# VectorE's tile loop in a group normalisation: from one tile per trip with addresses in registers to six slots per trip with fixed addresses

One core of one Trainium2 chip runs the kernel. The metric is the device time of one execution in microseconds (us). The kernel is hand-scheduled: each engine has its own program, and semaphores tie them together.

## The reference

Group normalisation of 128 samples, 1024 channels in 32 groups, 32 x 16 pixels, in bf16:

```python
xr = x.reshape(B, G, C // G, H, W)                       # 128, 32, 32, 32, 16
mu = xr.mean(axis=(2, 3, 4), keepdims=True)
var = ((xr - mu) ** 2).mean(axis=(2, 3, 4), keepdims=True)
xn = (xr - mu) / jnp.sqrt(var + 1e-5)
return xn.reshape(B, C, H, W) * g[None, :, None, None] + b[None, :, None, None]
```

## The kernel before

A tile is four samples: 128 partitions (sample and group) x 16384 elements, 4.19 MB. There are 32 tiles and a ring of six slots in SBUF. A tile is loaded into its slot, reduced, normalised in place and stored. SyncE issues every load and store into one queue, in batches (RUNS): some stores, then as many loads into the slots that they free. TensorE adds up the first half of a tile in PSUM; VectorE adds up the second half in one instruction (the *pair sum*); ScalarE turns both into the mean, squares the tile and makes the standard deviation; VectorE inverts it, makes scale and bias for 32 channels and runs 32 multiplies over the tile.

VectorE's program, the part that is changed, is a loop with one tile per trip. The slot depends on the trip, so the addresses are computed into registers:

```python
def part(i, lo, n):
    at = (i % SLOTS) * (F * ITEM) + lo * ITEM
    return bytes_of_ring[:, bass.ds(at, n * ITEM)].bitcast(BF16)

def pair(i):
    e.wait_ge(first_in, i + 1)                # TensorE's first matmul of tile i
    e.scalar_tensor_tensor(out=jp[:], in0=part(i, lo, n), scalar=1.0, in1=part(i, lo + n, n),
        ..., accum_out=ps[:, bass.ds((i % PS_BUFS) * (2 * MM_FREE) + MM_FREE, 1)]).then_inc(paired, 1)
...
pair(0)
with nc.Fori(0, NT, 1, engines=[e.engine]) as i:
    with e.If(i < NT - 1):
        e.drain()
        pair(i + 1)                           # one tile ahead
    parts = [part(i, k * HW, HW) for k in range(KC)]
    e.wait_ge(stded, i + 1)                   # ScalarE
    e.reciprocal(out=rstd[:], in_=std[:, bass.ds(i % SLOTS, 1)]).then_inc(inverted, 1)
    ...                                       # scale, bias
    for k, a in enumerate(parts):             # 32 multiplies
        ts = e.tensor_scalar(out=a, in0=a, ...)
        if (k + 1) % KQ == 0:
            ts.then_inc(done, 1)              # four times a tile; SyncE's stores wait for it
```

SyncE's stores and loads, unchanged:

```python
def load(j):
    if j >= SLOTS:
        e.wait_ge(st[j % SLOTS], ...)         # the store that frees the slot has landed
    e.dma_start(out=slot(j), in_=x_v[j]).then_inc(ld[j % SLOTS], 16)
def store(i):
    w = F // store_parts(i)                   # one part; two for tile 2, four for the last
    for p in range(store_parts(i)):
        e.wait_ge(done, NQ * i + NQ // store_parts(i) * (p + 1))
        e.dma_start(out=o_v[i][:, p * w : (p + 1) * w], in_=slot(i)[:, p * w : (p + 1) * w]).then_inc(...)
```

Of the kernel before, what the change touches and what calls it, by code (L numbers as in the profile page):

```python
# [8 lines left out]
ALU = mybir.AluOpType  # L9
F32 = mybir.dt.float32  # L10
BF16 = mybir.dt.bfloat16
# [5 lines left out]
SLOTS = 6  # L17
RUNS = (3, 4, 4, 4, 4, 4, 3, 6)
NQ = 4
PS_BUFS = 3  # L20
PE_CHUNKS = 16
MM_FREE = 512
# [35 lines left out]
def kernel(  # L58
# [13 lines left out]
    nc = tc.nc  # L72
# [3 lines left out]
    HW = H * W  # L76
# [3 lines left out]
    NT = B0 // NS  # L80
    KC = C // G
    F = KC * HW
    inv_n = 1.0 / float(F)
    NMM = F // MM_FREE
    ROUNDS = -(-NT // SLOTS)
    REST = NT - (ROUNDS - 1) * SLOTS
    KQ = KC // NQ
    PAIRED = F - PE_CHUNKS * MM_FREE
    ITEM = 2
# [8 lines left out]
    def sbuf(name, shape, dtype):  # L98
        return nc.alloc_sbuf_tensor(name, shape, dtype)


    ring = sbuf("ring", [P, SLOTS * F], BF16)
    ja = sbuf("ja", [P, F // 2], FP8)
    jm = sbuf("jm", [P, MM_FREE + 1], FP8)
    jp = sbuf("jp", [P, PAIRED // 2], FP8)
# [4 lines left out]
    gb = sbuf("gb", [P, 2 * KC], F32)  # L110
    eps_t = sbuf("eps_t", [P, 1], F32)
    warm = sbuf("warm", [P, 1], F32)
    nm = sbuf("nm", [P, SLOTS], F32)
    sq = sbuf("sq", [P, 2], F32)
    var = sbuf("var", [P, 1], F32)
    std = sbuf("std", [P, SLOTS], F32)
    rstd = sbuf("rstd", [P, 1], F32)
    scl = sbuf("scl", [P, KC], F32)
    bia = sbuf("bia", [P, KC], F32)

    ps = nc.alloc_psum_tensor("ps", [P, PS_BUFS * 2 * MM_FREE], F32)
    gb_p = nc.alloc_psum_tensor("gb_p", [P, 2 * KC], F32)

    def sem(name):
        return nc.alloc_semaphore(name)

    def sems(name):
        return [sem(f"{name}{c}") for c in range(SLOTS)]

    ld, st, summed, meaned = (sems(n) for n in ("ld", "st", "sum", "mean"))  # L130

    half, both, varred = (sems(n) for n in ("half", "both", "var"))
    inverted, scaled, shifted = (sem(n) for n in ("inv", "scl", "bia"))
    first_in, paired, stded, done = (sem(n) for n in ("first", "pair", "std", "done"))
    s_gb, s_ones, s_eye, s_gbp, s_fin = (sem(n) for n in ("gbl", "ones", "eye", "gbp", "fin"))

    def store_parts(i):
# [2 lines left out]
    def slot(i):  # L140
        return ring[:, (i % SLOTS) * F : (i % SLOTS + 1) * F]

    def sums(c):
        return ps[:, c % PS_BUFS * 2 * MM_FREE : c % PS_BUFS * 2 * MM_FREE + MM_FREE]

    def sums_and_pairs(c):
        return ps[:, c % PS_BUFS * 2 * MM_FREE : c % PS_BUFS * 2 * MM_FREE + MM_FREE + 1]
# [49 lines left out]
    def in_rounds(e, one):  # L197
        with nc.Fori(0, ROUNDS, 1, engines=[e.engine]) as t:
            for c in range(REST):
                one(c, t)  # L200
            with e.If(t < ROUNDS - 1):
                for c in range(REST, SLOTS):
                    one(c, t)

    def on_tensor(e):
        e.wait_ge(s_eye, 2)
        e.wait_ge(s_gb, 32)
        e.matmul(out=gb_p[:], lhsT=rep[:], rhs=gb_b[:], start=True, stop=True).then_inc(s_gbp, 1)  # L208

        e.ldweights(eye[:])  # L210

        def add_up(to, chunk, k):
            return e.add_instruction(  # L213
                mybir.InstMatmult(
                    name=nc.get_next_instruction_name(),
                    engine=e.engine,
                    start_tensor_calc=(k == 0),
                    stop_tensor_calc=(k == PE_CHUNKS - 1),
                    ins=[e.lower_ap(chunk), e.lower_ap(eye[:])],
                    outs=[e.lower_ap(to)],  # L220
                    tile_size=(P, P),
                    tile_position=(0, 0),
                    ldweights=False,
                )
            )

        def one(c, t):
            for k in range(PE_CHUNKS):
                if k == 0:
                    e.wait_ge(ld[c], (t + 1) * 16)  # L230
                elif k == PE_CHUNKS - 2:

                    e.wait_ge(meaned[(c - 2) % SLOTS], t + 1)
                elif k == PE_CHUNKS - 1:
                    e.wait_ge(paired, t * SLOTS + (c + 1))
                mm = add_up(sums(c), slot(c)[:, k * MM_FREE : (k + 1) * MM_FREE], k)
                if k == 0:
                    mm.then_inc(first_in, 1)
            mm.then_inc(summed[c], 1)

        in_rounds(e, one)

    def on_scalar(e):
        e.dma_start(out=gb_b[:, 0:KC], in_=g_v).then_inc(s_gb, 16)
        e.dma_start(out=gb_b[:, KC : 2 * KC], in_=b_v).then_inc(s_gb, 16)
        e.wait_ge(s_ones, 1)
        e.activation(out=warm[:], in_=eps_t[:], func=ACT.Sqrt)  # L247

        def one(c, t):
            e.wait_ge(summed[c], t + 1)  # L250
            e.activation(  # L251
                out=jm[:], in_=sums_and_pairs(c), func=ACT.Identity, scale=-inv_n,
                accum_out=nm[:, c : c + 1], saturate=False,
            ).then_inc(meaned[c], 1)
            for h, (ready, at) in enumerate(
                ((meaned[c], t + (2 if c >= SLOTS - 2 else 1)), (half[c], t + 1))
            ):
                e.wait_ge(ready, at)
                e.activation(  # L259
                    out=ja[:],  # L260
                    in_=slot(c)[:, h * (F // 2) : (h + 1) * (F // 2)],
                    func=ACT.Square,
                    bias=nm[:, c : c + 1],
                    scale=1.0,
                    accum_out=sq[:, h : h + 1],
                    saturate=False,
                ).then_inc((half, both)[h][c], 1)
            e.wait_ge(both[c], t + 1)
            e.activation(  # L269
                out=var[:], in_=sq[:, 0:1], func=ACT.Identity, bias=eps_t[:], scale=inv_n  # L270
            ).then_inc(varred[c], 1)
            e.wait_ge(varred[c], t + 1)
            e.activation(  # L273
                out=std[:, c : c + 1], in_=sq[:, 1:2], func=ACT.Sqrt, bias=var[:], scale=inv_n
            ).then_inc(stded, 1)

        in_rounds(e, one)

    def on_vector(e):
        bytes_of_ring = ring[:].bitcast(mybir.dt.uint8)  # L280

        def part(i, lo, n):
            at = (i % SLOTS) * (F * ITEM) + lo * ITEM
            return bytes_of_ring[:, bass.ds(at, n * ITEM)].bitcast(BF16)

        def pair(i):
            lo, n = PE_CHUNKS * MM_FREE, PAIRED // 2
            e.wait_ge(first_in, i + 1)
            e.scalar_tensor_tensor(  # L289
                out=jp[:],  # L290
                in0=part(i, lo, n),
                scalar=1.0,
                in1=part(i, lo + n, n),
                op0=ALU.mult,
                op1=ALU.add,
                accum_out=ps[:, bass.ds((i % PS_BUFS) * (2 * MM_FREE) + MM_FREE, 1)],
                saturate=False,
            ).then_inc(paired, 1)

        e.wait_ge(s_gbp, 1)  # L300
        e.tensor_copy(out=gb[:], in_=gb_p[:])  # L301
        pair(0)
        with nc.Fori(0, NT, 1, engines=[e.engine]) as i:
            with e.If(i < NT - 1):
                e.drain()  # L305
                pair(i + 1)
            parts = [part(i, k * HW, HW) for k in range(KC)]
            e.keepalive_nop([e.lower_ap(a) for a in parts])  # L308
            e.wait_ge(stded, i + 1)
            e.reciprocal(out=rstd[:], in_=std[:, bass.ds(i % SLOTS, 1)]).then_inc(inverted, 1)  # L310
            e.wait_ge(inverted, i + 1)
            e.tensor_scalar(  # L312
                out=scl[:], in0=gb[:, 0:KC], scalar1=rstd[:], scalar2=None, op0=ALU.mult
            ).then_inc(scaled, 1)
            e.wait_ge(scaled, i + 1)
            e.scalar_tensor_tensor(  # L316
                out=bia[:], in0=scl[:], scalar=nm[:, bass.ds(i % SLOTS, 1)],
                in1=gb[:, KC : 2 * KC], op0=ALU.mult, op1=ALU.add,
            ).then_inc(shifted, 1)
            e.wait_ge(shifted, i + 1)  # L320
            for k, a in enumerate(parts):
                ts = e.tensor_scalar(  # L322
                    out=a, in0=a, scalar1=scl[:, k : k + 1], scalar2=bia[:, k : k + 1],
                    op0=ALU.mult, op1=ALU.add,
                )
                if (k + 1) % KQ == 0:
                    ts.then_inc(done, 1)

    with entry_block(tc) as entry:
        first_load(nc.sync)  # L330
# [3 lines left out]
        at = next(k for k, i in enumerate(rest) if is_drain(i) and i.engine == load_0.engine)  # L334
# [36 lines left out]
```

## Time and profile before

| | before |
|---|---|
| time, median of the first three runs | 630.68 us (630.53 to 631.03) |
| span in the profile | 629.1 us |
| DMA queue that carries the data | 268.44 MB, 99.3% of the engines' time |
| VectorE, ScalarE, TensorE busy | 497.2, 504.0, 187.5 us |

The profile's lines are shown in the prediction. In a line of groups or of the timeline, "busy" counts the engine alone; registers, branches, drains and waits of its sequencer are not in it. A row with a "q" behind the engine (DVEq, SPq) is such sequencer work. "A <- B" in a view of waits says what ended A's wait.

### The profile page before, as it was taken

Reading aid. Unit: us, or ns where it says so; the run is one execution under the profiler, and the core shown is the slowest. Engines: PE = TensorE matmul, PEld = TensorE weight load, DVE = VectorE, ACT = ScalarE, POOL = GpSimd, SP = SyncE. Lnnn points to the kernel's source line nnn. Section 1 sums busy time; section 2 is a strip of 40 time slices with the busy share of each in tenths; the row PEclk is TensorE's granted clock in tenths of the full one; section 3 lists DMA queues with packets and bytes.
Section 4 is the critical chain, followed back from the end, with each engine's and each line's share of the span. In section 5 each row is a group of like instructions: output and inputs, shape, how many; then the busy total and the mean of one; then the engine's idle time right before and its main releaser. Section 6 shows DMA issues by size and latency. Waiting matters only on the chain.

```text
span 629.1 us, 2702 instructions
## 1 busy us (share of the span) xinstructions
PE 187.5 (30%) x508; PEld 0.2 (0%) x2; DVE 497.2 (79%) x1185; ACT 504.0 (80%) x258; POOL 1.0 (0%) x8
## 2 busy tenths in 40 slices
PE   2533333430243303433024330343303333063000
PEld 0000000000000000000000000000000000000000
DVE  1479999999499982999829998299983999899962
ACT  0899999999589992999929999299991999979940
POOL 0000000000000000000000000000000000000000
PEclk9867766665577755777557775577755866577555
DMA  9999999999999999999999999999999999999996
GB/s 400 433 433 400 433 433 433 433 433 433 431 433 433 433 433 433 433 425 433 433 433 433 433 431 433 433 433 433 433 433 433 433 431 431 433 427 433 433 419 270
DMA packets 9888, 268.44 MB, mean 427 GB/s; under 512 B 1184, under 2 KB 1184, under 8 KB 1184
## 3 DMA queue, kind: packets, MB, share of 16 engines
q1 hardware_dynamic: 9792, 268.44, 99.3%
q10 hardware_dynamic: 96, 0.00, 0.0%
HBM read 134.22 MB, written 134.22 MB: 427 GB/s over the span
## 4 chain that ended last, share of the span: by engine, by line
ACT 32%; DVE 25%; DMA 24%; issue 9%; PE 4%; DVEq 3%; SPq 0%; ACTq 0%
ACT ja L259 30%; DVE ring L322 23%; DMA ring<-in_x_dram 22%; PE ps L213 4%; DMA gb_b<-in_b_dram 2%; ACT jm L251 1%; DVEq L305 1%; DVEq L308 1%; DVE jp L289 1%; ACT var L269 1%; ACT std L273 1%; DVE bia L316 1%; DVE scl L312 1%; DVEq L289 0%; DVE rstd L310 0%
## 5 line engine op out<-in xcount | busy, mean ns | idle before, releaser
L259 ACT ACTIVATE ja<-ring,nm 128x8192 fp8e5<-128x8192 bf16 x64 | 455.8, 7122 | 2.1
L322 DVE TENSOR_SCALAR ring<-ring,scl,bia x1024 | 333.7, 409 | 1.2
L213 PE MATMUL ps<-ring,eye 128*128 128x512 bf16 x507 | 187.3, 543 | 389.3 <-DVE jp L289 235.1
L289 DVE SCALAR_TENSOR_TENSOR jp<-ring 128x4096 fp8e5 (+1 forms) x32 | 141.6, 4425 | 80.9 <-PE ps L213 68.9
L251 ACT ACTIVATE jm<-ps 128x513 fp8e5<-128x513 f32 x32 | 19.2, 601 | 95.3 <-PE ps L213 95.3
L310 DVE RECIPROCAL rstd<-std 128x1 f32 x32 | 5.7, 177 | 19.3 <-ACT std L273 19.2
L259 ACT ACTIVATION_READ_ACCUMULATOR ja<-ring,nm 128x1 f32 x64 | 11.9, 186 | 0.0
L316 DVE SCALAR_TENSOR_TENSOR bia<-scl,nm,gb 128x32 f32<-128x32 f32 x32 | 8.0, 251 | 4.2
L301 DVE COPY gb<-gb_p 128x64 f32<-128x64 f32 x1 | 0.2, 225 | 12.8 <-PE gb_p L208 12.8
L273 ACT ACTIVATE std<-sq,var 128x1 f32<-128x1 f32 x32 | 9.4, 294 | 1.0
L269 ACT ACTIVATE var<-sq,eps_t 128x1 f32<-128x1 f32 x32 | 9.4, 295 | 1.0
L312 DVE TENSOR_SCALAR scl<-gb,rstd 128x32 f32<-128x32 f32 x32 | 7.7, 242 | 1.1
L251 ACT ACTIVATION_READ_ACCUMULATOR jm<-ps 128x1 f32 x32 | 6.2, 194 | 0.0
L289 DVE DVE_READ_ACCUMULATOR jp<-ring (+1 forms) x32 | 4.5, 142 | 0.0
L208 PE MATMUL gb_p<-gb_b,rep 32*128 32x64 bf16 x1 | 0.2, 208 | 12.5 <-DMA gb_b<-in_b_dram 12.5
L247 ACT ACT_TABLE_LOAD x1 | 1.3, 1283 | 1.8 <-PEq L355 1.8
L190 POOL TENSOR_SCALAR_AFFINE_SELECT rep<-ones_b 32x128 bf16<-32x128 bf16 x1 | 0.3, 303 | 0.0
L186 POOL TENSOR_SCALAR_AFFINE_SELECT eye<-ones_b 128x128 bf16<-128x128 bf16 x1 | 0.3, 293 | 0.4 <-issue 0.4
L247 ACT ACTIVATE warm<-eps_t 128x1 f32<-128x1 f32 x1 | 0.2, 203 | 0.0
L180 POOL MEMSET ones_b<- 128x128 bf16 x1 | 0.2, 204 | 0.3 <-POOLq L355 0.3
L210 PEld LDWEIGHTS <-eye 128*128 128x128 bf16 x1 | 0.1, 105 | 0.1
L208 PEld LDWEIGHTS gb_p<-gb_b,rep 32*128 32x128 bf16 x1 | 0.1, 100 | 12.5 <-issue 12.5
(5 smaller groups left out, 0.5 us busy)
## 6 DMA issues: line engine op xcount, KB each, us to landing
ring<-in_x_dram SPq DMA_DIRECT2D x32, 4096.0 KB, 36.8
out_dram<-ring SPq DMA_DIRECT2D x30, 4096.0 KB, 26.9
out_dram<-ring SPq DMA_DIRECT2D x2, 2048.0 KB, 12.5
out_dram<-ring SPq DMA_DIRECT2D x4, 1024.0 KB, 9.2
gb_b<-in_g_dram ACTq DMA_DIRECT2D x1, 2.0 KB, 7.8
gb_b<-in_b_dram ACTq DMA_DIRECT2D x1, 2.0 KB, 11.1
```

Source lines behind the costliest of these rows:

```text
L213: return e.add_instruction(mybir.InstMatmult(name=nc.get_next_instruction_name(), engine=e.engine, start_tensor_calc=(k == 0), stop_tensor ...
L251: e.activation(out=jm[:], in_=sums_and_pairs(c), func=ACT.Identity, scale=-inv_n, accum_out=nm[:, c : c + 1], saturate=False,).then_inc(me ...
L259: e.activation(out=ja[:], in_=slot(c)[:, h * (F // 2) : (h + 1) * (F // 2)], func=ACT.Square, bias=nm[:, c : c + 1], scale=1.0, accum_out= ...
L269: e.activation(out=var[:], in_=sq[:, 0:1], func=ACT.Identity, bias=eps_t[:], scale=inv_n).then_inc(varred[c], 1)
L273: e.activation(out=std[:, c : c + 1], in_=sq[:, 1:2], func=ACT.Sqrt, bias=var[:], scale=inv_n).then_inc(stded, 1)
L289: e.scalar_tensor_tensor(out=jp[:], in0=part(i, lo, n), scalar=1.0, in1=part(i, lo + n, n), op0=ALU.mult, op1=ALU.add, accum_out=ps[:, bas ...
L305: e.drain()
L308: e.keepalive_nop([e.lower_ap(a) for a in parts])
L310: e.reciprocal(out=rstd[:], in_=std[:, bass.ds(i % SLOTS, 1)]).then_inc(inverted, 1)
L312: e.tensor_scalar(out=scl[:], in0=gb[:, 0:KC], scalar1=rstd[:], scalar2=None, op0=ALU.mult).then_inc(scaled, 1)
L316: e.scalar_tensor_tensor(out=bia[:], in0=scl[:], scalar=nm[:, bass.ds(i % SLOTS, 1)], in1=gb[:, KC : 2 * KC], op0=ALU.mult, op1=ALU.add,). ...
L322: ts = e.tensor_scalar(out=a, in0=a, scalar1=scl[:, k : k + 1], scalar2=bia[:, k : k + 1], op0=ALU.mult, op1=ALU.add,)
```

## The change

The intent is to take loop overhead off VectorE: with one trip per *round* of six slots every address is a constant, so that the drain and the register arithmetic ahead of each tile can go. Each slot then has semaphores of its own, counted once per round. The pair sum also waits for the load itself instead of for TensorE's first matmul. Cut to its core:

```diff
-        def pair(i):
-            lo, n = PE_CHUNKS * MM_FREE, PAIRED // 2
-            e.wait_ge(first_in, i + 1)
+        def pair(c, turn):
+            first, w = PE_CHUNKS * MM_FREE, PAIRED // 2
+            e.wait_ge(ld[c], turn * 16)
             e.scalar_tensor_tensor(
                 out=jp[:],
-                in0=part(i, lo, n),
+                in0=slot(c)[:, first : first + w],
 ... (in1 and accum_out alike)
-            ).then_inc(paired, 1)
-        with nc.Fori(0, NT, 1, engines=[e.engine]) as i:
-            with e.If(i < NT - 1):
-                e.drain()
-                pair(i + 1)
-            parts = [part(i, k * HW, HW) for k in range(KC)]
-            e.keepalive_nop([e.lower_ap(a) for a in parts])
-            e.wait_ge(stded, i + 1)
-            e.reciprocal(out=rstd[:], in_=std[:, bass.ds(i % SLOTS, 1)]).then_inc(inverted, 1)
+            ).then_inc(paired[c], 1)
+        def one(c, t):
+            then = (c + 1) % SLOTS, t + (1 + (c + 1) // SLOTS)
+            if c == REST - 1:
+                with e.If(t < ROUNDS - 1):
+                    pair(*then)
+            else:
+                pair(*then)
+            e.wait_ge(stded[c], t + 1)
+            e.reciprocal(out=rstd[:], in_=std[:, c : c + 1]).then_inc(inverted[c], 1)
 ... (scale, bias and the 32 multiplies alike, with slot(c) for the register address)
+        in_rounds(e, one)      # a loop over six rounds, six slots in each
 ... (TensorE: the wait for `paired` per slot, `first_in` is gone; ScalarE: semaphores per slot)
```

More of the change, by code (lines that the diff above doesn't have):

```diff
@@ L128, in sems @@
         return [sem(f"{name}{c}") for c in range(SLOTS)]
-    ld, st, summed, meaned = (sems(n) for n in ("ld", "st", "sum", "mean"))
-    half, both, varred = (sems(n) for n in ("half", "both", "var"))
-    inverted, scaled, shifted = (sem(n) for n in ("inv", "scl", "bia"))
-    first_in, paired, stded, done = (sem(n) for n in ("first", "pair", "std", "done"))
+    ld, st, summed, paired, meaned, stded = (
+        sems(n) for n in ("ld", "st", "sum", "pair", "mean", "std")
+    )
+    half, both, varred, inverted, scaled, shifted = (
+        sems(n) for n in ("half", "both", "var", "inv", "scl", "bia")
+    )
+    done = sem("done")
     s_gb, s_ones, s_eye, s_gbp, s_fin = (sem(n) for n in ("gbl", "ones", "eye", "gbp", "fin"))
@@ L234, in one @@
                 elif k == PE_CHUNKS - 1:
-                    e.wait_ge(paired, t * SLOTS + (c + 1))
+                    e.wait_ge(paired[c], t + 1)
                 mm = add_up(sums(c), slot(c)[:, k * MM_FREE : (k + 1) * MM_FREE], k)
-                if k == 0:
-                    mm.then_inc(first_in, 1)
             mm.then_inc(summed[c], 1)
@@ L254, in one @@
             ).then_inc(meaned[c], 1)
-            for h, (ready, at) in enumerate(
-                ((meaned[c], t + (2 if c >= SLOTS - 2 else 1)), (half[c], t + 1))
-            ):
-                e.wait_ge(ready, at)
+            e.wait_ge(meaned[c], t + (2 if c >= SLOTS - 2 else 1))
+            for h in range(2):
+                if h == 1:
+                    e.wait_ge(half[c], t + 1)
                 e.activation(
@@ L266, in one @@
                     saturate=False,
-                ).then_inc((half, both)[h][c], 1)
+                ).then_inc(both[c] if h == 1 else half[c], 1)
             e.wait_ge(both[c], t + 1)
@@ L274, in one @@
                 out=std[:, c : c + 1], in_=sq[:, 1:2], func=ACT.Sqrt, bias=var[:], scale=inv_n
-            ).then_inc(stded, 1)
+            ).then_inc(stded[c], 1)
         in_rounds(e, one)
     def on_vector(e):
-        bytes_of_ring = ring[:].bitcast(mybir.dt.uint8)
-        def part(i, lo, n):
-            at = (i % SLOTS) * (F * ITEM) + lo * ITEM
-            return bytes_of_ring[:, bass.ds(at, n * ITEM)].bitcast(BF16)
-        def pair(i):
-            lo, n = PE_CHUNKS * MM_FREE, PAIRED // 2
-            e.wait_ge(first_in, i + 1)
+        e.wait_ge(s_gbp, 1)
@@ L289, in pair @@
+        e.tensor_copy(out=gb[:], in_=gb_p[:])
+        def pair(c, turn):
+            first, w = PE_CHUNKS * MM_FREE, PAIRED // 2
+            e.wait_ge(ld[c], turn * 16)
             e.scalar_tensor_tensor(
                 out=jp[:],
-                in0=part(i, lo, n),
+                in0=slot(c)[:, first : first + w],
                 scalar=1.0,
-                in1=part(i, lo + n, n),
+                in1=slot(c)[:, first + w : first + 2 * w],
                 op0=ALU.mult,
                 op1=ALU.add,
-                accum_out=ps[:, bass.ds((i % PS_BUFS) * (2 * MM_FREE) + MM_FREE, 1)],
+                accum_out=ps[:, c % PS_BUFS * 2 * MM_FREE + MM_FREE :][:, 0:1],
@@ L297, in pair @@
                 saturate=False,
-            ).then_inc(paired, 1)
-        e.wait_ge(s_gbp, 1)
-        e.tensor_copy(out=gb[:], in_=gb_p[:])
-        pair(0)
-        with nc.Fori(0, NT, 1, engines=[e.engine]) as i:
-            with e.If(i < NT - 1):
-                e.drain()
-                pair(i + 1)
-            parts = [part(i, k * HW, HW) for k in range(KC)]
-            e.keepalive_nop([e.lower_ap(a) for a in parts])
-            e.wait_ge(stded, i + 1)
-            e.reciprocal(out=rstd[:], in_=std[:, bass.ds(i % SLOTS, 1)]).then_inc(inverted, 1)
-            e.wait_ge(inverted, i + 1)
+            ).then_inc(paired[c], 1)
@@ L312, in on_vector @@
+        def one(c, t):
[7 more added lines that the diff above has]
+            e.reciprocal(out=rstd[:], in_=std[:, c : c + 1]).then_inc(inverted[c], 1)
+            e.wait_ge(inverted[c], t + 1)
             e.tensor_scalar(
                 out=scl[:], in0=gb[:, 0:KC], scalar1=rstd[:], scalar2=None, op0=ALU.mult
-            ).then_inc(scaled, 1)
@@ L315, in on_vector @@
-            e.wait_ge(scaled, i + 1)
+            ).then_inc(scaled[c], 1)
+            e.wait_ge(scaled[c], t + 1)
             e.scalar_tensor_tensor(
-                out=bia[:], in0=scl[:], scalar=nm[:, bass.ds(i % SLOTS, 1)],
-                in1=gb[:, KC : 2 * KC], op0=ALU.mult, op1=ALU.add,
-            ).then_inc(shifted, 1)
-            e.wait_ge(shifted, i + 1)
-            for k, a in enumerate(parts):
+                out=bia[:], in0=scl[:], scalar=nm[:, c : c + 1], in1=gb[:, KC : 2 * KC],
+                op0=ALU.mult, op1=ALU.add,
+            ).then_inc(shifted[c], 1)
@@ L322, in on_vector @@
+            e.wait_ge(shifted[c], t + 1)
+            for k in range(KC):
+                a = slot(c)[:, k * HW : (k + 1) * HW]
                 ts = e.tensor_scalar(
@@ L327, in on_vector @@
                     ts.then_inc(done, 1)
+        pair(0, 1)
+        e.wait_ge(paired[0], 1)
+        in_rounds(e, one)
     with entry_block(tc) as entry:
```

## The prediction

Statements on the hardware that no trace of this case shows are cut from the recorded text. Of rival (b), instruction fetches, how many packets a jump might fetch and the time worked out from that are cut too; "the worst of (b)" further down is that estimate, and it was not shown. No term of the sum is cut: it came to 14 to 17 us off VectorE's elapsed work and 0.0 on the path that sets the end, so 630.7 us. The range around it, 629.3 to 632.5, rested in part on the cut estimate.

> **What bounds the kernel now.** I read the page first (busy shares, the 40 slices, the DMA queue), then the waits of the issuing engine, then single stretches of the timeline, and last the landings of each transfer. From the page of the kernel before:
>
> ```profile
> PE 187.5 (30%) x508; PEld 0.2 (0%) x2; DVE 497.2 (79%) x1185; ACT 504.0 (80%) x258; POOL 1.0 (0%) x8
> ...
> DMA  9999999999999999999999999999999999999996
> GB/s 400 433 433 400 433 433 433 433 433 433 431 433 433 433 433 433 433 425 433 433 433 433 433 431 433 433 433 433 433 433 433 433 431 431 433 427 433 433 419 270
> ...
> q1 hardware_dynamic: 9792, 268.44, 99.3%
> ...
> ACT 32%; DVE 25%; DMA 24%; issue 9%; PE 4%; DVEq 3%; SPq 0%; ACTq 0%
> ```
>
> VectorE and ScalarE are 80% busy and look like a co-bound, but the one queue that carries every load and store is 99.3% busy, and 433 GB/s comes back in slice after slice as a ceiling would. The program must move 268.44 MB; at 433 GB/s that is 620.0 us of a 629.1 us span. The chain that ended last names ACT and DVE for over half of the span, and this is the trap of this profile: it follows the releasers of instructions, and a store in a full queue is "released" by VectorE long before it moves.
>
> So the question is whether the queue ever runs dry because VectorE is late. The waits of the issuing engine:
>
> ```profile
> SPq L164 <- DVE ring L322: 472.9, 31, 42.4
> SPq L158 <- DMA out_dram<-ring: 112.0, 15, 9.6
> ```
>
> It waits 472.9 us for VectorE, yet the queue stays full. The trace shows why: each transfer records sixteen landings, one for each DMA engine. I took the eighth as its landing and compared each issue with the landing of the transfer ahead of it. Landings follow one another at 9.7 us (4.19 MB at 433 GB/s), and the queue still holds work at every issue after the first. The thinnest moments are the last store of each batch: issued at 144.7 us with 3.85 us of work ahead; 218.6 with 7.4; 375.7 with 5.6; 453.7 with 5.0; 600.2 with 3.75. The last quarter store is issued at 617.0 with 3.98 us ahead. Never under 3.7 us: VectorE could be 3 us later in any batch, or arbitrarily earlier, and no byte would move at another time.
>
> The end, from the DMA share of 1 us stretches (last two columns, share and GB/s):
>
> ```profile
> 616.00:617.00 1.00, 0.00 (x0) 0.00 (x0) 0.64 (x2) 0.00 (x0) 0.00 (x0) 0.50 1.02 434
> ...
> 622.00:623.00 1.00, 0.00 (x0) 0.00 (x0) 0.00 (x0) 0.00 (x0) 0.00 (x0) 0.50 0.91 385
> 623.00:624.00 1.00, 0.00 (x0) 0.00 (x0) 0.00 (x0) 0.00 (x0) 0.00 (x0) 0.50 0.22 90
> ...
> 627.00:628.00 1.00, 0.00 (x0) 0.00 (x0) 0.00 (x0) 0.00 (x0) 0.00 (x0) 0.50 0.04 16
> ```
>
> Full rate until 623, after VectorE's last instruction at 616.6; then a trickle until 628. The landings say what the trickle is: of the last transfer, fifteen engines land between 623.05 and 625.67 and one at 628.09. That one has fallen behind gradually (0.1 us behind the next at 70 us, 1.0 at 246, 2.1 at 330, 3.1 at 480). So the time is: first packets at 1.0, 620 to 622 of transfer, 2.4 to 5 of one lagging engine, and 1 of closing, 629.1; the measured 630.68 lies 1.6 above the span.
>
> [...]a 32 KB packet takes 1.213 us, which is 16 x 32768 / 1.213 = 432 GB/s. [...] The kernel before shows no instruction packet in its span up to 629.5 us, so it pays nothing of the kind; whether the changed one does is the second rival.
>
> **The change part by part.** The stretch of one tile on VectorE before:
>
> ```profile
> 202.41 4.43 DVE L289 SCALAR_TENSOR_TENSOR jp<-ring 128x4096 fp8e5 x1 [0.50 <-issue]
> 206.76 0.14 DVE L289 DVE_READ_ACCUMULATOR jp<-ring  x1
> 206.95 0.17 DVE L310 RECIPROCAL rstd<-std 128x1 f32 x1
> ```
>
> and its loop overhead, by line:
>
> ```profile
> DVE jp L289 <- issue: 12.0, 24, 0.5
> L305 DVEq DRAIN  x31: 3475/3494/4287, 13.6 to 580.3; - x31
> L289 DVEq FUSED_REGOPS  x62: 115/126/136, 22.5 to 584.0; - x62
> L308 DVEq FUSED_REGOPS  x192: 76/93/133, 22.9 to 597.2; - x192
> ```
>
> 1. Drain and address arithmetic ahead of the pair sum are removed. The drain's 3.49 us are mostly spent beside the multiplies still queued; what the engine loses is the 0.50 us gap: 24 x 0.50 = 12.0 us in all (the other pair sums wait for TensorE or a load anyway). With fixed addresses the next instruction is already queued, so I expect the 0.02 to 0.05 us that other neighbours show. Saving about 0.45 us a tile, 32 x 0.45 = 14 us at most.
> 2. The six register operations ahead of the reciprocal (6 x 0.093 = 0.56 us) run at 218.8 to 219.6 in one tile, under a pair sum that runs until 223.2. Saved: nothing. One more ahead of the reciprocal (0.05) and one ahead of the bias (0.04) are exposed: some 0.1 us a tile.
> 3. The pair sum waits for its load itself instead of for TensorE's first matmul of the tile. It can start about 0.7 us earlier in the 8 tiles where it is the load that is late (VectorE waited 68.9 us in these). They are already ahead of the queue by 20 to 36 us.
> 4. TensorE loses one register operation per tile before its last matmul, and ScalarE swaps semaphores: hundredths of a us.
> 5. The instructions that do the work are the same in number and shape, so VectorE stays at about 497 us busy; its cycle in a compute-limited batch falls from 16.6 us (185.81 to 202.41, pair sum to pair sum) to about 16.1. The queue needs 2 x 9.7 = 19.4 us a tile.
>
> Sum: 14 to 17 us come off VectorE's elapsed work, all of it in waiting that lies beside a full queue. The thinnest moments should thicken by about 0.5 us for each tile of a batch, 3.8 becoming 5 to 6. Transfers, their order in the single queue and their sizes are unchanged. On the path that sets the end: 0.0, with a few tenths of a us to either side from the lagging engine.
>
> **The rivals.** (a) VectorE's saving reaches the end: 630.7 - 14 = 617 us, 2.2% faster. For it speak the chain of waits and the 472.9 us; against it the 3.7 us of work always queued, and the floor: 1.0 + 620.0 + 2.4 + 1 is already 624. The head (the first load is issued at 0.00, before VectorE does anything) and the tail (queue full to 623) are both beyond its reach. At best a smaller lag gives 2 to 3 us. (b) Instruction fetches. VectorE's program grows from 111 to 240 instructions as built, a loop of some 225. [...] Packets of this kind outside the span took 0.3 to 0.55 us. [...] I hold it for unlikely, but it skews the range upward. (c) The lag itself moves: it differs by engine[...], and could be 3 or 7 us instead of 5, so 628.5 to 633. The three times before lie within 0.5 us, so it repeats on one chip and program.
>
> **Range and chances.** The middle is the time before, 630.7. From (c) and (b) together I take 629.3 to 632.5. Faster by 2% would be under 618.1, below the 624 just worked out: 1%. Slower by 2% is over 643.3, past even the worst of (b): 1%. Within 2%: 98%.
>
> **What would show it right or wrong.** Right: the 433s in the slices stay, the queue is 99% busy; VectorE's pair sums lose their 0.50 us "issue" gap and the drain row goes; its busy time stays near 497; its idle time moves into waits for ScalarE and for loads; the work ahead of each last store of a batch grows by 1 to 2 us; the last landing stays near 628. Wrong: a slice below 400 between the first and the last (a starved queue), instruction packets inside the span with VectorE gaps of over 1 us every sixth tile, or a last landing that moves by more than 2 us.

## The result

Over six runs of each, the changed kernel took 630.84 us (630.54 to 631.14) and the kernel before 630.70 us (630.51 to 631.59). The ratio is 1.000, with a 95% interval of 0.9987 to 1.0013: the same. Ratios here are the mean time of one kernel's fast runs over that of the other's of the same rounds, so not quite the ratio of the medians that are quoted.

The page of the changed kernel, the lines that answer to those of before:

```profile
PE 183.0 (29%) x508; PEld 0.2 (0%) x2; DVE 495.6 (79%) x1185; ACT 503.0 (80%) x258; POOL 1.0 (0%) x8
...
GB/s 400 433 432 400 433 431 434 433 433 433 433 433 431 433 433 431 433 433 433 431 433 433 433 433 433 433 433 431 431 433 433 433 433 433 433 433 433 433 421 260
...
q1 hardware_dynamic: 9792, 268.44, 99.2%
...
q14 instruction: 2, 0.02, 0.0%
...
DMA 35%; ACT 35%; DVE 20%; PE 6%; issue 1%; SPq 0%; DVEq 0%; ACTq 0%
```

The queue is as full as it was. In the chain "issue" fell from 9% to 1% and DVEq from 3% to 0%. VectorE's drains ahead of the pair sum are gone from the trace, and its waits list no "issue" ahead of the pair sum any more (12.0 us before): the loop overhead is gone. The q14 line, packets that fetch instructions, is new. Three lines of the timeline, VectorE in the same stretch as in the prediction:

```profile
203.28 4.41 DVE L288 SCALAR_TENSOR_TENSOR jp<-ring 128x4096 fp8e5<-128x4096 bf16 x1
207.63 0.13 DVE L288 DVE_READ_ACCUMULATOR jp<-ring 128x1 f32 x1
...
224.31 0.16 DVE L308 RECIPROCAL rstd<-std 128x1 f32<-128x1 f32 x1 [0.82 <-ACT std L275]
```

The pair sum no longer has "[0.50 <-issue]" behind it. The reciprocal of the next tile now waits 0.82 us for ScalarE. The waits tell where the rest went, first VectorE's, then the issuing engine's:

```profile
DVE jp L288 <- DMA ring<-in_x_dram: 73.0, 7, 13.2
DVE rstd L308 <- ACT std L275: 29.1, 18, 8.0
```

```profile
SPq L168 <- DVE ring L321: 461.2, 30, 42.6
SPq L162 <- DMA out_dram<-ring: 121.8, 15, 9.4
SPq L181 <- DMA out_dram<-ring: 13.3, 1, 13.3
```

VectorE's waits for ScalarE grew from 19.2 to 29.1 us. SyncE waits 11.7 us less for VectorE, and 9.8 us more for landings of stores ahead of its loads, where it waited 112.0. The last store was handed over earlier and waits longer for its landing (13.3 us where it was 11.1). In short: a faster VectorE hands its stores to a queue that is just as long.

How long the queue is at each issue can be worked out from the trace: the landing of the transfer ahead (the median of its sixteen engines) minus the time at which the issue is done. At the thinnest moments, the last store of a batch (the batch of three near 515 us, with over 10 us in both, is left out), the last whole tile near 600, and the last quarter:

| issued at about (us) | 144 | 218 | 296 | 375 | 453 | 600 | last quarter, 617 |
|---|---|---|---|---|---|---|---|
| before, us of work ahead | 3.9 | 7.5 | 7.0 | 5.6 | 5.0 | 3.8 | 4.0 |
| after | 6.0 | 6.6 | 5.9 | 5.0 | 4.4 | 4.8 | 5.8 |

It never runs dry in either kernel.

### The profile page after: what moved, and what is told of

Same layout as the page of the kernel before. It is cut to its first block, busy times and chain, and to the rows that moved or that the text cites. A ratio compares the mean times of both kernels' runs of the same rounds, so it can differ in the third digit from the quotient of the medians.

```text
span 629.4 us, 2165 instructions
## 1 busy us (share of the span) xinstructions
PE 183.0 (29%) x508; PEld 0.2 (0%) x2; DVE 495.6 (79%) x1185; ACT 503.0 (80%) x258; POOL 1.0 (0%) x8
## 3 DMA queue, kind: packets, MB, share of 16 engines
q1 hardware_dynamic: 9792, 268.44, 99.2%
## 4 chain that ended last, share of the span: by engine, by line
DMA 35%; ACT 35%; DVE 20%; PE 6%; issue 1%; SPq 0%; DVEq 0%; ACTq 0%
ACT ja L261 32%; DMA ring<-in_x_dram 23%; DVE ring L321 16%; DMA out_dram<-ring 11%; PE ps L217 6%; DVE jp L288 3%; DMA gb_b<-in_b_dram 2%; ACT jm L253 1%; ACT var L271 1%; ACT std L275 1%; DVE bia L314 0%; DVE scl L310 0%; DVE rstd L308 0%; SPq L168 0%; DVEq L369 0%
## 5 line engine op out<-in xcount | busy, mean ns | idle before, releaser
L321 DVE TENSOR_SCALAR ring<-ring,scl,bia 128x512 bf16<-128x512 bf16 x1024 | 333.5, 406 | 1.2
L217 PE MATMUL ps<-ring,eye 128*128 128x512 bf16 x507 | 182.8, 533 | 392.3 <-DVE jp L288 220.3
L288 DVE SCALAR_TENSOR_TENSOR jp<-ring 128x4096 fp8e5<-128x4096 bf16 x32 | 141.4, 4418 | 73.0 <-DMA ring<-in_x_dram 73.0
L253 ACT ACTIVATE jm<-ps 128x513 fp8e5<-128x513 f32 x32 | 19.1, 596 | 94.7 <-PE ps L217 94.7
L308 DVE RECIPROCAL rstd<-std 128x1 f32<-128x1 f32 x32 | 5.4, 170 | 30.2 <-ACT std L275 29.1
L288 DVE DVE_READ_ACCUMULATOR jp<-ring 128x1 f32 x32 | 4.5, 139 | 0.0
L212 PE MATMUL gb_p<-gb_b,rep 32*128 32x64 bf16 x1 | 0.2, 207 | 12.5 <-DMA gb_b<-in_b_dram 12.5
## 6 DMA issues: line engine op xcount, KB each, us to landing
gb_b<-in_b_dram ACTq DMA_DIRECT2D x1, 2.0 KB, 11.1
```

Of the source, the lines that this page charges most:

```text
L217: return e.add_instruction(mybir.InstMatmult(name=nc.get_next_instruction_name(), engine=e.engine, start_tensor_calc=(k == 0), stop_tensor ...
L253: e.activation(out=jm[:], in_=sums_and_pairs(c), func=ACT.Identity, scale=-inv_n, accum_out=nm[:, c : c + 1], saturate=False,).then_inc(me ...
L288: e.scalar_tensor_tensor(out=jp[:], in0=slot(c)[:, first : first + w], scalar=1.0, in1=slot(c)[:, first + w : first + 2 * w], op0=ALU.mult ...
L308: e.reciprocal(out=rstd[:], in_=std[:, c : c + 1]).then_inc(inverted[c], 1)
L321: ts = e.tensor_scalar(out=a, in0=a, scalar1=scl[:, k : k + 1], scalar2=bia[:, k : k + 1], op0=ALU.mult, op1=ALU.add,)
```

## The experiments

Theory Q: the always full DMA queue sets the time and hides whatever VectorE saves; what VectorE may lose or gain is told by the thinnest moment of that queue. Rivals: P, VectorE is on the path and some new cost ate its saving; S, ScalarE, equally busy, takes the saving as a wait; N, nothing was saved. A further theory, F, came from the q14 line: instruction packets hold up a DMA engine.

### Half of every tile stored

To see VectorE's saving one must take the queue out of the way. Both kernels with half stores; the results are wrong (half of the output is never written):

```diff
-    out=o_v[i][:, p * w : (p + 1) * w], in_=slot(i)[:, p * w : (p + 1) * w]
+    out=o_v[i][:, p * w : p * w + w // 2], in_=slot(i)[:, p * w : p * w + w // 2]
```

> The kernel before with half of each tile stored (wrong on purpose): 201.3 MB instead of 268.4, at 433 GB/s 465 us, so the queue should no longer bound. Theory Q (the full queue hides VectorE): the queue's share falls to about 0.83 and the loop of VectorE and ScalarE sets the time, 34 us of head + 31 x 16.6 + some 19 of tail = about 568 us. Taken with the next run it tells Q from its rivals.

> The changed kernel with half of each tile stored (wrong on purpose). Theory Q: with the queue out of the way the 0.45 to 0.5 us a tile appear, 14 to 16 us faster than the same half store of the kernel before (about 553 against 568, 2.5 to 3%). Rival S (ScalarE, as busy, would take the saving as VectorE's wait for it even without the queue): under 5 us. Rival N (the change saves nothing at all, an expected saving misread from the trace): 0 us.

Measured: 565.42 us (565.04 to 566.65) with the loop of before, 555.49 (552.58 to 555.69) with the changed one, 0.8963 and 0.8793 of the full kernel before beside them: 9.9 us apart in the medians, 1.9% by the ratios. Both were run again on another chip:

> The kernel before with half stores once more, for comparison on the same chip: 565 to 567 us as before, 10 us above the changed one.

> The changed kernel with half stores once more, for comparison on the same chip: 552.5 to 556 us as before.

Measured: 565.55 (565.23 to 565.74) and 554.42 (554.18 to 555.07), 11.1 us apart. The saving is real, so N falls. It appears only when the queue is not full, which is Q, though it is smaller than the 14 to 16 us that Q expected; P falls with it, as no new cost is there to eat it. Of the queue, and of VectorE's groups (busy, mean ns, then idle before and its releasers), with the loop of before:

```profile
q1 hardware_dynamic: 9792, 201.33, 84.9%
```

```profile
L289 DVE SCALAR_TENSOR_TENSOR jp<-ring 128x4096 fp8e5 (+1 forms) x32 | 141.6, 4426 | 26.0 <-PE ps L213 13.6 <-issue 12.5
L316 DVE SCALAR_TENSOR_TENSOR bia<-scl,nm,gb 128x32 f32<-128x32 f32 x32 | 8.0, 251 | 4.2
...
L310 DVE RECIPROCAL rstd<-std 128x1 f32 x32 | 5.5, 173 | 18.8 <-ACT std L273 18.4
```

and with the changed one, half stores both:

```profile
L288 DVE SCALAR_TENSOR_TENSOR jp<-ring 128x4096 fp8e5<-128x4096 bf16 x32 | 141.7, 4428 | 8.8 <-DMA ring<-in_x_dram 8.8
L314 DVE SCALAR_TENSOR_TENSOR bia<-scl,nm,gb 128x32 f32<-128x32 f32 x32 | 8.0, 251 | 1.1
...
L308 DVE RECIPROCAL rstd<-std 128x1 f32<-128x1 f32 x32 | 5.4, 170 | 29.8 <-ACT std L275 28.5
```

The idle time ahead of these three falls by 17.2 (26.0 to 8.8) and 3.1 (4.2 to 1.1), and grows by 11.0 (18.8 to 29.8) ahead of the reciprocal: 9.3 us net. So S is right in part: without the queue, ScalarE takes about half of what VectorE sheds. The trace shows how, in the first tiles, where no load is late. With the loop of before, ScalarE starts a tile every 16.17 and 16.77 us by turns; with the changed one every 15.74 and 16.39. It is itself busy for 503.0 / 32 = 15.7 us a tile, so every second tile is now at ScalarE's own floor. VectorE's mean cycle falls by 0.40 us there, from 16.47 to 16.07.

### Which part of the change saves what

The kernel before with half stores, without its drain; registers and shared semaphores stay:

```diff
         with e.If(i < NT - 1):
-            e.drain()
             pair(i + 1)
```

> The kernel before with half stores and without its explicit drain ahead of the pair sum; registers and shared semaphores stay. Theory D (the drain is what exposes the register operations: behind it they can start only when the multiplies are done, without it they run beside them): the 0.50 us gap goes, and 8 to 11 of the 9.9 us between the two half-store kernels come back: 555 to 557 us. Rival R (the register operations themselves hold the engine up, drain or no drain): at most 3 us, 562 to 565.

Measured: 560.18 us (559.77 to 561.13), so 5.2 of the 9.9 us come from the drain alone (it ran on another chip than these two kernels), between the two theories. The groups:

```profile
L289 DVE SCALAR_TENSOR_TENSOR jp<-ring 128x4096 fp8e5 (+1 forms) x32 | 141.6, 4426 | 13.8 <-PE ps L213 13.8
L315 DVE SCALAR_TENSOR_TENSOR bia<-scl,nm,gb 128x32 f32<-128x32 f32 x32 | 8.0, 251 | 4.2
...
L309 DVE RECIPROCAL rstd<-std 128x1 f32 x32 | 5.4, 169 | 26.0 <-ACT std L273 25.5
```

The mechanism of theory D is right: all of the 12.5 us of "issue" are gone, though every register operation is still there. Of the 62 ahead of the pair sum, 50 now run while the engine is busy, and with the drain none did. The size was wrong, because the reciprocal's wait for ScalarE grew by 7.2 us (18.8 to 26.0). The bias keeps its 4.2 us: its register operation is still ahead of it. One more part, the wait, put back into the changed kernel with half stores:

```diff
+                if k == 0:
+                    mm.then_inc(first_in[c], 1)
 ...
-            e.wait_ge(ld[c], turn * 16)
+            e.wait_ge(first_in[c], turn)
```

> The changed kernel with half stores, whose pair sum waits again for TensorE's first matmul of the tile (a semaphore per slot) instead of for the load. Open after the run without the drain: 4.7 us between 560.2 and 555.5. Theory W (the longer wait costs about 0.6 us wherever a load is late, 5 to 7 times): 558.5 to 560 us. Rival G (the rest is the register operations ahead of the reciprocal and the bias, 0.1 us a tile, about 3 us): within 1 us of the changed kernel with half stores run beside it.

Measured: 556.74 us (556.28 to 556.92) against 554.42 beside it, so the wait for TensorE is worth 2.3 us: less than W said, more than G. What is left between 560.18 and 556.74, 3.4 us from two chips, fits the register operations ahead of the reciprocal and the bias; that remainder was not run by itself.

### VectorE made slower again

Into the changed kernel, an idle fill of 960 or 2880 elements in each tile (with a wait for the pair sum after each pair sum, left out here, so that the fill is free of races; the profile puts 7.1 us of idle time down to this wait):

```diff
             e.wait_ge(stded[c], t + 1)
+            e.memset(jp[:, 0:960], 1.0)        # 2880 in the second
             e.reciprocal(...)
```

> The changed kernel with one idle fill of 960 elements (about 1.0 us) on VectorE in each tile ahead of the reciprocal, twice what the change saves. Theory Q: the work queued ahead of the last store of the first batches falls by about 6 us there and 2 to 3 later, to 0 to 3 us, and the time stays at 630.8 within 1 us. Rival P (VectorE on the path): 32 x 1.0 = +32 us, 663.

Measured: 630.86 us (630.71 to 631.69), the ratio to the kernel before 1.0002 (0.9987 to 1.0017). The fill took 0.86 us and put VectorE's cycle at about 16.6, a little over that of the kernel before:

```profile
L310 DVE MEMSET jp<- 128x960 fp8e5 x32 | 27.5, 858 | 25.4 <-ACT std L275 18.3 <-DVE jp L288 7.1
```

The thinnest moments were 1.8 us at 146, 3.3 at 456 and 2.1 at 602: thinner than in either kernel, still not dry, and no time lost. P would have had 32 x 0.86 = 27 us by the fill, or 32 x 0.5 = 16 by the longer cycle (16.6 instead of 16.07). The larger fill:

> The changed kernel with an idle fill of 2880 elements (about 2.8 us; the fill of 960 took 0.86) on VectorE in each tile, which makes its cycle about 18.6 us, still under the queue's 19.4. Theory Q (what counts is the thinnest moment of the queue, not the mean): the first batches have 6 us ahead at 142 us and seven tiles of 2.5 us each before that, so the queue runs dry there by about 11 us, later batches by 0 to 3 us each and the end by some 3 us: 15 to 25 us slower, 646 to 656 us, with slices under 400 GB/s near 140 us. Rival A (an average bound: 18.6 is under 19.4, so nothing changes): 631. Rival P (VectorE on the path throughout): 32 x 2.5 = +80 us.

Measured: 651.34 us (649.75 to 652.61), 3.4% slower, inside the expected 15 to 25 us. The rate per fortieth of the span:

```profile
GB/s 389 449 425 419 390 411 431 403 405 210 407 427 415 453 421 427 447 421 441 431 419 425 417 429 445 423 443 413 437 421 423 449 407 435 421 441 433 427 271 376
```

In the slice with 210 (146 to 162 us) the queue ran dry: the last store of the first batches came 7.9 us after the work ahead of it had landed. The 271 is the store of the tile before the last, issued 5.4 us late. Between 200 and 600 us the thinnest moments are 1.5 to 2.4 us. A dry moment costs more than its 7.9 or 5.4 us: these two stores landed 19.3 and 16.1 us after the transfer ahead of them, where it was 10.1 and 9.7 in the kernel before. In all, the last transfer's median landing is 23.6 us later (647.1 instead of 623.5). The last of its sixteen landings is only 19.1 us later (647.2 instead of 628.1), because the engine that lagged by 4.6 us before has caught up. VectorE's cycle was then 18.6 us, less than the 19.4 that the queue needs for a tile, so the rival that compares averages is wrong too: the starved moments are at the ramp and at the end, where no work had been built up ahead.

### VectorE's program written out

The changed kernel's trace has two instruction packets of 8 KB in its span, at 46.9 and 104.1 us; the kernel before has none. In the kernel before, one DMA engine falls behind the others little by little. In the changed one another engine gains 0.8 and 1.0 us of lag in the two transfers that were moving when these packets came, and that one lands last. (The records do not name the engines; which is which is read from the steady order of the landings. It gains another 0.8 near 59 us, where the trace has no instruction packet, only one data packet of 2.9 us; that step is not explained.) Lag is here the last of a transfer's sixteen landings minus their median:

| transfer landing at about (us) | 41 | 61 | 110 | 245 | 352 | 449 | 604 | end of the last landing |
|---|---|---|---|---|---|---|---|---|
| before | 0.3 | 0.4 | 0.4 | 1.4 | 2.6 | 3.4 | 4.5 | 628.09 |
| after | 0.3 | 2.0 | 3.0 | 3.3 | 4.1 | 4.5 | 5.4 | 628.58 |
| after, the second to last engine | 0.2 | 0.3 | 0.3 | 1.2 | 2.5 | 3.2 | 4.3 | |
| written out (below) | 0.2 | 1.5 | 2.4 | 4.3 | 5.0 | 6.6 | 8.5 | 631.58 |

The third row follows the first: that engine still lags as it did and is now second to last. To test it, the 32 tiles were written out, about 1,200 instructions without a loop:

```diff
-        in_rounds(e, one)
+        for i in range(NT):
+            one(i % SLOTS, i // SLOTS)
 ... (the test for the last tile is now made when the program is built)
```

> The changed kernel with VectorE's 32 tiles written out, about 1,200 instructions in a row instead of a loop of 225; everything else equal. Theory F (each 8 KB instruction packet holds up one DMA engine by about 0.9 us, as the two in the changed kernel's trace seem to, and the last engine sets the end): 8 to 9 packets in the span, the lag of that engine grows from 5.4 to about 11 to 12 us, and the time to 636 to 638 us (+1%). Rival (instruction packets do not matter): 630.8 us, within 0.5.

Measured: 634.40 us (634.21 to 634.54), the ratio to the kernel before 1.0059 (1.0045 to 1.0073): slower by 3.7 us. From its page and from its 2 us stretches (last columns: DMA share, GB/s):

```profile
q14 instruction: 9, 0.07, 0.0%
```

```profile
626.00:628.00 2.00, 0.00 (x0) 0.00 (x0) 0.00 (x0) 0.00 (x0) 0.00 (x0) 0.50 0.08 33
628.00:630.00 2.00, 0.00 (x0) 0.00 (x0) 0.00 (x0) 0.00 (x0) 0.00 (x0) 0.50 0.06 25
630.00:632.00 2.00, 0.00 (x0) 0.00 (x0) 0.00 (x0) 0.00 (x0) 0.00 (x0) 0.50 0.04 16
```

Nine packets of about 0.31 us each; the lag steps up at each of them, from 0.2 to 8.6 us, so (8.6 - 0.2) / 9 = 0.93 us a packet. Most of that can be seen in the packets: the data packet that begins where an instruction packet ends takes 1.57 to 1.88 us, 1.76 on average, where the usual one takes 1.21, and 0.31 + 0.55 = 0.86 us. The second to last engine has landed by 626.9, and one works on until 631.6. A queue that ran dry is not the cause: the median landing of the last transfer is at 623.4, where it was at 623.5 in the kernel before. VectorE itself does not stall: its waits for loads and for ScalarE, 74.3 and 31.2 us, are close to those of the changed kernel (73.0 and 29.1). F holds, though 636 to 638 was too much: I had put seven more packets on top of a lag of 5.4 us, of which only two or three steps came again; the slow drift that this engine had in the changed kernel did not. Why the data packet behind a fetch takes longer, and what the drift of the other engine is, stays open. All six runs with the changed loop show two such packets in the span, and none of the five with the loop of before shows any. In these runs lag lasted only where the queue did not empty: with half stores and the changed loop it rose to 1.5 us or more by 115 us and was 0.4 or less from 133 us on (0.6 or less there in every run with half stores), and with the fill of 2880 it fell to 0.1 after each of the two dry moments.

### Less work for one engine at the end

In the kernel before, the last two quarter stores were split by partitions, to leave one engine out (the edit is shortened here):

```diff
+                rows = ((0, 120), (120, P)) if i == NT - 1 and p >= 2 else ((0, P),)
+                for a, z in rows:
+                    e.dma_start(out=o_v[i][a:z, ...], in_=slot(i)[a:z, ...])
```

> The kernel before with the last two quarter stores each split into 120 and 8 partitions, so that one of the sixteen DMA engines should get nothing of them (about 4.9 us less work) and eight others 0.6 us more. [...] If the engine that lags here is the one left out: the last landing comes 2 to 2.5 us earlier, 628.3 us. If it is another: 630.7 to 631.3 us, nothing or slightly worse.

Measured: 635.12 us (634.98 to 635.32), 0.7% slower: a miss, and more so than its second case allowed. The packets fit the intended split: the data queue has 9,806, where the kernel before has 9,792, of which 8,704 move data. The 66 unsplit transfers have 16 completions each, so 9,806 - 8,704 - 66 x 16 = 46 are left, 23 for each of the two split stores: this fits fifteen engines for the 120 rows and eight for the 8. In the trace the last data packet moves at 632.05 to 632.36, behind a completion of its own. That packet, between two completions, is the row of the 8-partition store, so the engine that ends last is one that got extra rows. That makes it unlikely that the one left out was the one that lagged. Which engine lags stays open, and so does the size of the loss: two extra rows are 0.6 us of work (an 8 KB packet takes 0.31 us in the kernel before), and the last landing came 4.6 us later (632.70 against 628.09). No correct version tried is faster than either kernel.

## Why the prediction was right

The time: 630.7 was predicted and 630.84 measured, because the first reading, that the queue is never dry when VectorE hands over a store, held in both kernels. With whole tiles stored, the time moved only where the queue did run dry (the larger fill), where fetches held up one DMA engine (the program written out), or where the last stores themselves were changed.

- *The drain and the gap of 0.50 us.* As predicted: the "issue" wait is gone and the run without the drain confirms the drain as what exposed the register operations.
- *Register operations.* The six ahead of the reciprocal cost nothing, as said; the exposed ones "some 0.1 us a tile", where the bias alone shows 3.1 / 32 = 0.10.
- *The wait for the load.* Said to let the pair sum start about 0.7 us earlier: it starts 0.03 us after the landing of a late load (at 170.82) where it was 0.99 (at 168.65). Worth 2.3 us where the queue is not full, nothing where it is.
- *VectorE's cycle,* said to fall from 16.6 to about 16.1 us, fell from 16.47 to 16.07. "14 to 17 us come off VectorE's elapsed work" was too much: freed of the queue the kernel gains 9.9 and 11.1 us. The term left out was ScalarE's floor of 15.7 us a tile. The sum was also generous: it put 0.45 us on 32 tiles where its own line counts 24 gaps (24 x 0.45 = 10.8).
- *"The thinnest moments should thicken by about 0.5 us for each tile of a batch."* Right for the first batches (3.9 to 6.0) and at the end (4.0 to 5.8), wrong in the four batches between, which became 0.6 to 1.1 us thinner. There VectorE first waits for a load, and a load is complete only when its last engine has landed. In the trace that is 170.82 us after and 168.65 before for the same load, 2.2 us later by the lag of the engine with the instruction packets; the pair sum starts at 170.85, not at 169.64.
- *Rival (b), instruction fetches.* Held for unlikely, and half true. The loop did not fetch at each lap: both packets, at 46.9 and 104.1 us, are in the first, and VectorE did not stall (none of its waits is an "issue"). But they fell on one DMA engine, which now lands last, at 628.58 instead of 628.09. That 0.5 us is within the scatter of the times; the 3.7 us of nine packets are not. That "the last landing stays near 628" came true is thus partly luck: another engine sets it, and it happened to end close to the old one.
- *The landings at the end.* Of the "fifteen engines" that land by 625.67, the last is misread: from 625.2 us a single stream of packets runs to 627.65, so 625.67 is the lagging engine's own landing of the quarter store before, and the others had landed by 625.2. The sum is not touched.
- *Rival (a), a saving that reaches the end,* is ruled out by both fills and by the half stores.

## What to carry to other kernels

Before an engine is made faster, look at whether the queue behind it ever runs dry: subtract each issue from the landing of the transfer ahead, and look at the smallest difference, not at busy shares or at the chain of waits. To find what an optimisation off the path is worth, thin out what binds (here half of the stores) and measure both kernels there. Here, with the DMA queue 99% busy, code size counted: each of the nine instruction packets of the program written out put about 0.93 us of lag on one DMA engine, that engine ended the kernel, and the time was 3.7 us above that of the kernel before.
